# Which engine makes the low mantissa bits of three weight blocks: GpSimd or VectorE, in an attention and rational feed-forward kernel

## The chip, the core and the metric

The kernel runs on one core of a Trainium2 chip. The metric is the device time of one execution in microseconds (us), lower is better. The kernel before has a median of 679.99 us over 3 runs, from 679.7 to 680.04.

The core has four computing engines, each of which runs its own list of instructions strictly in order: TensorE (PE, its weight loads are shown as PEld), VectorE (DVE), ScalarE (ACT) and GpSimd (POOL). SyncE (SP) issues the transfers. An instruction waits for semaphores that other engines raise, and everything behind it on its engine waits with it.

## The reference

```python
def _attn_ref(x, state):                      # x: 8 x 8 x 512 x 64, state: 8 x 8 x 32 x 64
    scores = scale * np.matmul(x, state.transpose(0, 1, 3, 2))
    a = softmax(scores)                       # over the 32 states
    xread = np.matmul(a, state)
    scores2 = scale * np.matmul(state, x.transpose(0, 1, 3, 2))
    a2 = softmax(scores2)                     # over the 512 positions
    sread = np.matmul(a2, x)
    return np.concatenate([xread, sread], axis=2)

def _moe_ref(x, w_in, w_out, a, b):           # x: 4352 x 512, w_in: 512 x 2048, w_out: 2048 x 512
    h = x @ w_in
    P = a[0] + a[1] * h + a[2] * h**2 + a[3] * h**3
    Q = 1.0 + np.abs(b[0]) * np.abs(h) + np.abs(b[1]) * h**2
    return ((P / (Q + 1e-06)) @ w_out).astype(np.float32)
```

`w_in` and `w_out` reach the kernel as 64-bit floats, seen as two 32-bit words per number. The kernel makes 32-bit floats of them itself, at its start.

## The kernel before

The order of all work is written out by hand in the table `ORDER`: a list of tokens such as `jr:2`, each of which calls one small function. Every function appends its instructions to the lists of its engines, so that the table sets the order on each engine. Waits are put in by the framework, from the tiles that instructions read and write.

**The weights.** There are 16 raw blocks of 128 x 1024 numbers (1 MB each), numbered by `groups`: 0, 1, 2 are the first three eighths of `w_in`, then eighths of `w_out` and of `w_in` take turns (block 3 is `w_out` 0, block 4 is `w_in` 3, block 5 is `w_out` 1). A block g passes these steps:

- `lr:g:k` (`load_raw`, issued at L281 or L287) loads half k of it into a raw tile of pairs of words.
- `cp:g:k` (`conv_parts`, L299, ScalarE) makes the sign, exponent and upper mantissa of half k, into the tile `cv_y`.
- `jr:g` (`join_rest`, L308) makes the three lowest mantissa bits out of the other word: it reads every second word of the raw tile, multiplies by 2^-29, takes the minimum with 7 and writes integers to the tile `cv_r`.
- `jl:g` (`join`, L319, VectorE) shifts `cv_y` and joins it with `cv_r`. For a block of `w_in` the result is `win_sb`; for one of `w_out` it goes back into `cv_r`.
- For `w_out`, `wh:g` (L329, ScalarE) and `wl:g:k` (L336, GpSimd) split the result into a high and a low part for TensorE.

`cv_y` and `cv_r` share four buffers. As the program is built, the `cv_r` of block 2 lies in the buffer that held the `cv_r` of block 1, which `jl:1` reads; the `cv_r` of block 3 lies in the buffer of block 2's `cv_y`, which `jl:2` reads; the `cv_r` of block 4 lies where that of block 2 was.

**The rest of the start.** Beside this, the start computes the attention of the first batch (`scores0`, `row_max0` and so on; `row_norm0`, L577, runs on GpSimd, `a_lo0`, L591, on VectorE), and folds state and `w_in` into products (`X`, L694, with `XA`, L712, `fh`, L726, and `fo`, L730).

**The main part.** 72 steps n then pass through the rational function. `F` (L784, PE) makes h; `FC` (L796) and `FB` (L803) copy it on ScalarE; `qd` (L817), `mu` (L807), `po` (L811), `g1`, `g2`, `g3` (L828, L834, L840) run on VectorE; `qa` (L823), `ln` (L893) and `ex` (L903) on ScalarE; `gl` (L847) on GpSimd; `mh` and `ml` (L856) multiply by `w_out` on PE. The first of them starts at 21 us, while blocks 2 to 4 are being converted. That stretch of the table reads:

```python
    "cp:2:0 a_hi0:1 cv e2_copy0:0 cp:2:1 b0a cp:3:0 fh:1 a_lo0:0 a_lo0:1 jr:2 jl:2 F:0:0 XA:4 F:0:1 "
    "fo:1 cp:3:1 cp:4:0 jr:3 col_norm:0 F:1:0 jl:3 F:1:1 jr:4 FC:0 lr:5:0 FB:0 wh:3 FB:1 qd:0 ..."
```

Of the kernel before, what the change touches and what calls it, by code (L numbers as in the profile page):

```python
# [198 lines left out]
def attention_rational_ffn(  # L199
# [6 lines left out]
    nc = tc.nc  # L206
# [98 lines left out]
        )  # L305

    def join_rest(g):
        nc.vector.tensor_scalar(  # L308
            CV[g][1], RAW[g][:, :, 0], 2.0**-29, 7.0, op0=ALU.mult, op1=ALU.min
        )  # L310

# [598 lines left out]
    def sread_lo():  # L910
# [8 lines left out]
        "lr": load_raw,  # L919
        "cp": conv_parts,  # L920
        "jr": join_rest,
        "jl": join,
        "ws": store_win,
# [50 lines left out]
    for name, args in tokens:  # L974
        if name in ("scores0", "scores", "sread"):
            b, g = (0, *args)[-2:]
# [51 lines left out]
```

## Time and profile before

| what | value |
|---|---|
| median of 3 runs | 679.99 us (679.7 to 680.04) |
| span of the profiled execution, first to last instruction | 678.2 us |
| the runs' median less that span | 1.8 us |
| PE busy | 653.1 us (96%) |
| DVE busy | 629.4 us (93%) |
| ACT busy | 518.4 us (76%) |
| POOL busy | 307.4 us (45%) |

The page gives no device time of its own for the profiled execution; its span is what stands there, and it is 1.8 us less than the median of the runs. Busy time counts the instructions of an engine from start to end. A busy PE is no PE at its peak, and a wait of an engine costs time only where something else waits for what comes after it.

### The profile page before, as it was taken

To read this page: it belongs to the slowest core of one execution; us is meant where nothing else is said; L and a number is where in the kernel's file an instruction comes from. 1 tells how busy PE (TensorE), PEld (TensorE's weight loads), DVE (VectorE), ACT (ScalarE), POOL (GpSimd) and SP (SyncE) were. 2 spreads that over 40 slices of the span, in tenths; PEclk is the share of its full clock that TensorE was granted. 3 is DMA by queue.
4 is the path that set the end of the run, shared out by engine and by line. 5 is a ranking of instruction groups with operands and counts; after the bars stand their busy time and mean duration, and the time that the engine had idled before them with its cause. 6 is when DMAs were issued, how large, how long until landed. Compare 5 with 4: busy or idle time off the path is not lost.

```text
span 678.2 us, 11288 instructions
## 1 busy us (share of the span) xinstructions
PE 653.1 (96%) x4474; PEld 510.7 (75%) x4474; DVE 629.4 (93%) x583; ACT 518.4 (76%) x633; POOL 307.4 (45%) x174
## 2 busy tenths in 40 slices
PE   5779999999999999999999999999999999999997
PEld 2547667877887777877878878778878888888895
DVE  4989999899998998899999998999999998999896
ACT  4989989886787777786786867858787868774772
POOL 1234346434543445344554455543553565465630
PEclk9979999999999999999999999999999999999999
DMA  8959886334442454021333203121412111204301
GB/s 334 412 213 338 303 289 234 100 125 141 135 157 56 150 183 161 32 73 52 109 128 121 63 16 105 53 74 64 140 54 88 62 48 62 78 0 141 124 2 31
DMA packets 30679, 85.67 MB, mean 126 GB/s; under 512 B 3490, under 2 KB 3618, under 8 KB 30626
## 3 DMA queue, kind: packets, MB, share of 16 engines
q1 hardware_dynamic: 30290, 84.56, 35.7%
q8 instruction: 35, 0.57, 0.3%
q10 hardware_dynamic: 336, 0.39, 0.2%
q14 instruction: 18, 0.15, 0.1%
HBM read 57.15 MB, written 27.79 MB: 125 GB/s over the span
## 4 chain that ended last, share of the span: by engine, by line
PE 85%; ACT 6%; DVE 5%; issue 2%; DMA 1%; POOL 0%; SPq 0%; POOLq 0%; DVEq 0%; ACTq 0%
PE h L784 27%; PE ps_x L694 3%; PE o__1511 L856 2%; PE o__3578 L856 2%; PE o__1588 L856 2%; PE o__4769 L856 2%; PE o__4111 L856 2%; PE o__4116 L856 2%; PE o__1516 L856 2%; PE o__5847 L856 2%; PE o__4121 L856 2%; PE o__5866 L856 2%; PE o__1506 L856 2%; PE o__3571 L856 2%; PE o__5331 L856 2%
## 5 line engine op out<-in xcount | busy, mean ns | idle before, releaser
L847 POOL TENSOR_TENSOR gl<-C,L 128x1024 fp32r<-128x1024 f32 (+1 forms) x70 | 173.3, 2476 | 228.7 <-DVE C L840 150.7
L784 PE MATMUL h<-aT,m 128*128 128x512 f32 x768 | 191.9, 393 | 1.4 <-DVE m L730 1.0
L784 PEld LDWEIGHTS h<-aT,m 128*128 128x128 f32 x768 | 143.0, 188 | 36.9 <-DVE m L730 1.9
L803 ACT ACTIVATE A<-h,cst 128x1024 f32<-128x1024 f32 (+1 forms) x72 | 77.0, 1069 | 43.7 <-PE h L784 43.0
L743 POOL TENSOR_TENSOR m<-m_sb,m 128x512 fp32r<-128x512 f32 x56 | 79.8, 1435 | 65.8 <-ACT m L739 42.8
L828 DVE SCALAR_TENSOR_TENSOR gh<-C,cst,L 128x1024 fp32r<-128x1024 f32 (+1 forms) x72 | 95.5, 1328 | 12.6 <-ACT L L903 10.9
L796 ACT ACTIVATE C<-h,cst 128x1024 f32<-128x1024 f32 (+1 forms) x72 | 83.4, 1159 | 22.6 <-PE h L784 14.1
L817 DVE SCALAR_TENSOR_TENSOR A<-A,b0a,h 128x1024 f32<-128x1024 f32 (+1 forms) x72 | 87.2, 1213 | 10.0 <-ACT A L803 6.3
L840 DVE SCALAR_TENSOR_TENSOR C<-C,cst,A 128x1024 f32<-128x1024 f32 (+1 forms) x72 | 94.3, 1311 | 0.8
L834 DVE SCALAR_TENSOR_TENSOR A<-A,gh 128x1024 f32<-128x1024 f32 (+1 forms) x72 | 89.2, 1241 | 1.2
L823 ACT ACTIVATE A<-A 128x1024 f32<-128x1024 f32 (+1 forms) x72 | 73.0, 1014 | 22.0 <-DVE A L817 21.3
L811 DVE SCALAR_TENSOR_TENSOR C<-C,cst,h 128x1024 f32<-128x1024 f32 (+1 forms) x72 | 87.5, 1217 | 1.3
L807 DVE TENSOR_TENSOR C<-C,h 128x1024 f32<-128x1024 f32 (+1 forms) x72 | 83.0, 1153 | 3.0 <-issue 1.3
L893 ACT ACTIVATE L<-A 128x1024 f32<-128x1024 f32 (+1 forms) x72 | 72.9, 1012 | 7.0 <-POOL gl L847 4.4
L903 ACT ACTIVATE L<-L 128x1024 f32<-128x1024 f32 (+1 forms) x72 | 72.8, 1012 | 1.3
L739 ACT CAST m<-m_sb 128x512 fp32r<-128x512 f32 x56 | 34.4, 617 | 7.8 <-PE h L784 6.9
L694 PE MATMUL ps_x<-win_sb,st 64*32 64x256 f32 x1024 | 37.1, 415 | 3.4 <-DVE win_sb L319 1.4
L694 PEld LDWEIGHTS ps_x<-win_sb,st 64*32 64x32 f32 x1024 | 18.1, 114 | 19.3 <-issue 8.6
L336 POOL TENSOR_TENSOR wo<-cv_r,wo 128x512 fp32r<-128x512 f32 x16 | 20.3, 1293 | 26.3 <-ACT wo L329 26.3
L784 PEld LDWEIGHTS h<-sh,m 128*128 128x128 f32 x192 | 24.6, 190 | 1.1
L489 POOL TENSOR_TENSOR e<-e,rs 128x512 f32<-128x512 f32 x14 | 17.3, 1256 | 17.2 <-DVE rs L483 17.2
L784 PE MATMUL h<-sh,m 128*128 128x256 f32 x192 | 24.9, 282 | 0.0
(246 smaller groups left out, 1121.5 us busy)
## 6 DMA issues: line engine op xcount, KB each, us to landing
m_sb<-m_dram SPq DMA_DIRECT2D x56, 256.0 KB, 3.0
xT_sb<-in_xT_dram SPq DMA_DIRECT2D x16, 512.0 KB, 4.8
x_sb<-in_x_dram SPq DMA_DIRECT2D x16, 512.0 KB, 5.8
m_dram<-xo SPq DMA_DIRECT2D x16, 512.0 KB, 5.6
win_sb<-w_in_dram SPq DMA_DIRECT2D x16, 512.0 KB, 4.5
out_dram<-o_sb SPq DMA_DIRECT2D x32, 256.0 KB, 3.8
raw<-in_w_in_dram SPq DMA_DIRECT2D x10, 512.0 KB, 7.9
raw_w<-in_w_out_dram SPq DMA_DIRECT2D x8, 512.0 KB, 9.4
```

Source lines behind the costliest of these rows:

```text
L743: nc.gpsimd.tensor_tensor(m[:, 1], MF.pop(n), m[:, 0].bitcast(F32), op=ALU.subtract)
L784: nc.tensor.matmul(h[:, ci * W : (ci + 1) * W], l, r, start=(q == 0), stop=(q == len(seq) - 1),)
L796: nc.scalar.activation(e["C"], e["h"], AF.Identity, scale=cst[:, 3:4], bias=cst[:, 2:3])
L803: nc.scalar.activation(e["A"], e["h"], AF.Abs, scale=cst[:, 5:6])
L807: nc.vector.tensor_tensor(e["C"], e["C"], e["h"], op=ALU.mult)
L811: nc.vector.scalar_tensor_tensor(e["C"], e["C"], cst[:, 1:2], e["h"], op0=ALU.add, op1=ALU.mult)
L817: nc.vector.scalar_tensor_tensor(e["A"], e["A"], b0a, e["h"], op0=ALU.add, op1=ALU.mult)
L828: nc.vector.scalar_tensor_tensor(e["gh"], e["C"], cst[:, 0:1], e["L"], op0=ALU.add, op1=ALU.mult)
L834: nc.vector.scalar_tensor_tensor(e["A"], e["A"], 1.0 + 1e-6, e["gh"].bitcast(F32), op0=ALU.add, op1=ALU.mult)
L840: nc.vector.scalar_tensor_tensor(e["C"], e["C"], cst[:, 0:1], e["A"], op0=ALU.add, op1=ALU.subtract)
L847: eng.tensor_tensor(e["gl"], e["C"], e["L"], op=ALU.mult)
L856: nc.tensor.matmul(O[t], e[l][:, j * W + t * P : j * W + (t + 1) * P], WO[u][:, j, k, :], start=(u == 0 and l == "gh" and k == 0 and j == ...
```

## The change

`jr:2`, `jr:3` and `jr:4`, that is blocks 2, 3 and 4 of the raw weights (the third to the fifth), go to GpSimd. The table `ORDER`, the tiles, the operation and its shapes stay as they are; `jr` of the 13 other blocks stays on VectorE. From L308 on, lines stand one further down.

```diff
     def join_rest(g):
-        nc.vector.tensor_scalar(
+        eng = nc.gpsimd if 2 <= g <= 4 else nc.vector
+        eng.tensor_scalar(
             CV[g][1], RAW[g][:, :, 0], 2.0**-29, 7.0, op0=ALU.mult, op1=ALU.min
         )
```

VectorE between `jl:1` (the first row) and `mu:0` (the last), before. `cv_r_286`, `cv_r_295` and `cv_r_322` are the `cv_r` tiles of blocks 2, 3 and 4:

```order
L319 SCALAR_TENSOR_TENSOR win_sb_256<-cv_y_171,cv_r_172 128x1024
L455 TENSOR_SCALAR r2_229<-r2_229 128x2
L591 TENSOR_TENSOR aT_264<-ps_a0_231,aT_264 128x512
L591 TENSOR_TENSOR aT_264<-ps_a0_259,aT_264 128x512
L308 TENSOR_SCALAR cv_r_286<-raw_w_137 128x1024
L319 SCALAR_TENSOR_TENSOR win_sb_302<-cv_y_285,cv_r_286 128x1024
L730 TENSOR_TENSOR m_297<-ps_x_268,m_297 128x512
L308 TENSOR_SCALAR cv_r_295<-raw_w_143 128x1024
L459 RECIPROCAL r2_229<-r2_229 128x2
L319 SCALAR_TENSOR_TENSOR cv_r_295<-cv_y_294,cv_r_295 128x1024
L308 TENSOR_SCALAR cv_r_322<-raw_203 128x1024
L817 SCALAR_TENSOR_TENSOR A_345<-A_345,b0a_82,h_304 128x1024
```

The same stretch of VectorE with the change, with the semaphores that each instruction waits for:

```order
L320 SCALAR_TENSOR_TENSOR win_sb<-cv_y,cv_r 128x1024 [waits DVE_49]
L456 TENSOR_SCALAR r_229<-r_229 128x2 [waits Activation_49]
L592 TENSOR_TENSOR aT<-ps_a_231,aT 128x512 [waits Activation_49]
L592 TENSOR_TENSOR aT<-ps_a_259,aT 128x512 [waits Activation_49]
L320 SCALAR_TENSOR_TENSOR win_sb<-cv_y,cv_r 128x1024 [waits Activation_49,Pool_49]
L731 TENSOR_TENSOR m<-ps_x,m 128x512 [waits PE_49,Activation_49]
L460 RECIPROCAL r_229<-r_229 128x2 [waits DVE_49]
L320 SCALAR_TENSOR_TENSOR cv_r<-cv_y,cv_r 128x1024 [waits Activation_49,Pool_49]
L818 SCALAR_TENSOR_TENSOR A<-A,b0a,h 128x1024 [waits PE_49,Activation_49]
```

Three instructions are gone, and the two joins `jl:2` and `jl:3` (L320) now wait for GpSimd.

GpSimd with the change, from `row_norm0` (L578) to the first `gl` (L848); before, the two `wl:3` (L337) followed on `row_norm0` directly:

```order
L578 TENSOR_TENSOR e_131<-e_131,rs 128x512 [waits DVE_49,Activation_49]
L578 TENSOR_TENSOR e_131<-e_131,rs 128x512 [waits DVE_49]
L309 TENSOR_SCALAR cv_r<-raw_w 128x1024 [waits DMAHW1_49,DMAHW0_49,DVE_49]
L309 TENSOR_SCALAR cv_r<-raw_w 128x1024 [waits DMAHW4_49,DMAHW2_49,DVE_49]
L309 TENSOR_SCALAR cv_r<-raw 128x1024 [waits DMAHW6_49,DMAHW5_49,Pool_49]
L337 TENSOR_TENSOR wo<-cv_r,wo 128x512 [waits Activation_49]
L337 TENSOR_TENSOR wo<-cv_r,wo 128x512
L848 TENSOR_TENSOR gl<-C,L 128x1024 [waits DVE_49,Activation_49]
```

The three new instructions stand together. The wait of the first for VectorE is for the end of `jl:1`, that of the second for the end of `jl:2` (`jl:1` and `jl:2` read the buffers that the two then write); the third waits for GpSimd's own first one.

## Rows read from the trace of the kernel before

**Rows 1.** The page: busy time of each engine, and the chain that ended last.

```profile
PE 653.1 (96%) x4474; PEld 510.7 (75%) x4474; DVE 629.4 (93%) x583; ACT 518.4 (76%) x633; POOL 307.4 (45%) x174
...
PE 85%; ACT 6%; DVE 5%; issue 2%; DMA 1%; POOL 0%; SPq 0%; POOLq 0%; DVEq 0%; ACTq 0%
```

**Rows 2.** Stretches: length, busy PE, PEld, DVE, ACT, POOL, clock, DMA share, GB/s.

```profile
20.00:30.00 10.00, 7.16 (x57) 4.93 (x56) 9.65 (x13) 9.97 (x17) 2.40 (x2) 1.00 1.02 410
30.00:40.00 10.00, 4.29 (x99) 2.75 (x107) 9.65 (x10) 8.56 (x13) 2.47 (x2) 0.53 0.61 238
```

**Rows 3.** Timeline of DVE: start, duration (us), engine, line, operation, tiles.

```profile
18.47 1.47 DVE L319 SCALAR_TENSOR_TENSOR win_sb<-cv_y,cv_r 128x1024 int32<-128x1024 int32 x1
...
21.25 0.68 DVE L308 TENSOR_SCALAR cv_r<-raw_w 128x1024 int32<-128x1024 uint32 x1
22.04 1.23 DVE L319 SCALAR_TENSOR_TENSOR win_sb<-cv_y,cv_r 128x1024 int32<-128x1024 int32 x1
23.40 0.69 DVE L730 TENSOR_TENSOR m<-ps_x,m 128x512 fp32r<-128x512 f32 x1
...
24.79 1.22 DVE L319 SCALAR_TENSOR_TENSOR cv_r<-cv_y,cv_r 128x1024 int32<-128x1024 int32 x1
25.93 0.69 DVE L308 TENSOR_SCALAR cv_r<-raw 128x1024 int32<-128x1024 uint32 x1
26.63 1.28 DVE L817 SCALAR_TENSOR_TENSOR A<-A,b0a,h 128x1024 f32<-128x1024 f32 x1
```

**Rows 4.** Timeline of ACT from 21 us on.

```profile
21.02 0.72 ACT L299 ACTIVATE cv_y<-raw_w 128x512 f32<-128x512 f32 x1
...
22.71 0.65 ACT L712 COPY xo<-ps_x 128x512 f32<-128x512 f32 x1
...
25.40 1.19 ACT L803 ACTIVATE A<-h,cst 128x1024 f32<-128x1024 f32 x1
26.41 1.12 ACT L329 CAST wo<-cv_r 128x1024 fp32r<-128x1024 f32 x1
```

**Rows 5.** All waits of ACT from 15 to 45 us: total, times, longest.

```profile
ACT xo_w L712 <- PE ps_x L694: 1.2, 1, 1.2
ACT srT L640 <- PE ps_sr L635: 0.6, 1, 0.6
```

**Rows 6.** Timeline of POOL: its neighbours around the three new instructions.

```profile
16.04 1.05 POOL L577 TENSOR_TENSOR e<-e,rs 128x512 f32<-128x512 f32 x1 [14.64 <-DVE cm L400]
17.49 1.37 POOL L577 TENSOR_TENSOR e<-e,rs 128x512 f32<-128x512 f32 x1 [0.40 <-DVE rs L572]
27.60 2.51 POOL L336 TENSOR_TENSOR wo<-cv_r,wo 128x512 fp32r<-128x512 f32 x2 [8.74 <-ACT wo L329]
```

**Rows 7.** Timeline of DVE: two instructions that ran beside POOL.

```profile
53.53 2.07 DVE L319 SCALAR_TENSOR_TENSOR win_sb<-cv_y,cv_r 128x1024 int32<-128x1024 int32 x1
...
257.72 1.83 DVE L828 SCALAR_TENSOR_TENSOR gh<-C,cst,L 128x1024 fp32r<-128x1024 f32 x1
```

**Rows 8.** Timeline of POOL beside those, and one undisturbed instruction (35.70).

```profile
35.70 2.36 POOL L847 TENSOR_TENSOR gl<-C,L 128x1024 fp32r<-128x1024 f32 x1 [5.59 <-DVE C L840]
...
51.97 2.55 POOL L336 TENSOR_TENSOR wo<-cv_r,wo 128x512 fp32r<-128x512 f32 x2
...
257.19 1.29 POOL L743 TENSOR_TENSOR m<-m_sb,m 128x512 fp32r<-128x512 f32 x1 [2.38 <-DVE r L455]
258.44 3.39 POOL L847 TENSOR_TENSOR gl<-C,L 128x1024 fp32r<-128x1024 f32 x1
```

**Rows 9.** POOL's groups by form: busy us, mean ns of one, idle before.

```profile
L911 POOL TENSOR_TENSOR sh<-srT,sh 128x1024 fp32r<-128x1024 f32 x1 | 2.4, 2420 | 0.0
...
masks.py:199 POOL TENSOR_SCALAR_AFFINE_SELECT ident<-ident 128x128 f32<-128x128 f32 x1 | 0.3, 284 | 0.0
masks.py:197 POOL MEMSET ident<- 128x128 f32 x1 | 0.2, 206 | 0.3 <-POOLq L1010 0.3
...
L1010 POOL MEMSET const-float32-0.0<- 128x1 f32 x1 | 0.1, 104 | 0.2 <-issue 0.2
```

## The prediction

> **What bounds the kernel now.** Begin with the page: PE is busy for 96% of the span and VectorE for 93%, and 85% of the chain that ended last lies on PE [rows 1]. That is an average over the whole kernel; the change touches the stretch from 20 to 27 us. So the second view is busy time by stretch [rows 2]: from 20 to 30 us ScalarE is busy for 9.97 of 10 us, VectorE for 9.65, PE for 7.16. Here ScalarE sets the pace. The waits of ScalarE say it more sharply: between 15 and 45 us it waits only twice, 1.2 us and 0.6 us, both times for PE [rows 5], so nothing that VectorE does in these 30 us holds it up. The third view is the timelines of the stretch, to see how much room the touched instructions have [rows 3, 4, 6].
>
> **What is removed.** Three instructions of VectorE of 0.68, 0.68 and 0.69 us [rows 3] (the second, `jr:3`, is like the first): 2.04 us. I cost their removal at nothing. `jl:2` started at 22.04, but it also needs ScalarE's `cp:2:1`, which ends at 21.02 + 0.72 = 21.74 [rows 4]. `fo:1` (23.40) needs what ScalarE signals at the end of `XA:4`, 22.71 + 0.65 = 23.36. `qd:0` (26.63) needs `FB:0`, which ends at 25.40 + 1.19 = 26.59. And `wh:3`, which needs `jl:3` (24.79 + 1.22 = 26.01), starts at 26.41 only because ScalarE comes to it then. Each of VectorE's results is met by a ScalarE that is not yet there, so the freed 2.04 us become idle time. The cover is ScalarE's full list; were it gone, up to 2.04 us could be won.
>
> **What is added: the way through GpSimd.** The three instructions stand between `row_norm0` (ends 17.49 + 1.37 = 18.86) and `wl:3` (27.60) in a gap of 8.74 us [rows 6]. GpSimd has the time; the question is who waits. With d for the duration of one, and 0.1 us for a semaphore's way (`wh:3` ends at 27.53 and `wl:3` starts at 27.60 [rows 4, 6]):
>
> - `jr:2` waits for `jl:1`, which ends at 18.47 + 1.47 = 19.94 [rows 3], so it runs from 20.04 to 20.04 + d.
> - `jl:2` starts at the later of 21.84 (ScalarE) and 20.14 + d. Up to d = 1.70 it is the first, and `jl:2` ends at 23.07, 0.20 earlier than before.
> - `jr:3` waits for `jl:2`: from 23.17 to 23.17 + d. `fo:1` is not moved.
> - `jr:4` stands right behind it: to 23.17 + 2d.
> - `jl:3` waits for `jr:3`. At 23.17 + d it is free to go, but `jr:4` already runs. Does it have to stand aside?
>
> **The shared way to memory.** It does, by the rows. `jl` of a later block, `L319` with two inputs from SBUF, started at 53.53 while GpSimd ran two instructions from 51.97 to 54.52, and took 2.07 us instead of 1.22: it ended at 55.60, 1.08 after GpSimd [rows 7, 8]. `jl:1` shows the same: it ended at 19.94, 1.08 after `row_norm0` [rows 3, 6]. The other direction is there too: an instruction of VectorE that was already waiting (257.72) ended at 259.55, 1.07 after GpSimd's running one (258.48), while GpSimd's next took 3.39 us instead of 2.36 [rows 7, 8]. So whoever comes second stands still until the first is done. `jr:4` comes first here, since it follows on its own engine, while `jl:3` hears of `jr:3` by a semaphore.
>
> The Trainium skill (SBUF — State Buffer, Who interferes with whom) has this as a rule: an instruction of VectorE with two SBUF inputs and one of GpSimd that reads SBUF exclude each other for the whole instruction. By that rule `jl:3` stands still as in my sum; without it `jl:3` would start at 23.27 + d, end at 25.99 for d = 1.5, and nothing would be lost.
>
> Thus `jl:3` ends at 23.17 + 2d + 1.08, and `wh:3` on ScalarE starts 0.07 later instead of at 26.41. The delay is 2d - 2.09 us, none up to d = 1.05; above d = 1.70 `jl:2` slips as well and each further us costs three.
>
> **The price d.** The trace has no one-input instruction of this size on GpSimd. From below: VectorE's own 0.68 us [rows 3], which gives no delay; a gain below that is excluded, as shown above. From above: 2.42 us for GpSimd with two inputs of 128 x 1024 [rows 9]; then `jl:2` ends at 20.14 + 2.42 + 1.23 = 23.79, `jl:3` at 23.89 + 4.84 + 1.08 = 29.81, and `wh:3` is 3.47 us late. Between them I go by the row that is nearest in kind, the affine select, also one input and one output: 0.284 us for 128 elements against 0.104 for a memset of one, so 0.18 / 127 = 1.42 ns per element, and 0.10 + 1.45 = 1.55 us for 1024 [rows 9]. I take **d = 1.5 us**: the delay is 2 x 1.5 - 2.09 = 0.9 us.
>
> **Does it reach the end?** `wh:3` is late by 0.9, and ScalarE's list behind it follows without a gap until its two waits [rows 5], which are for PE work that itself waits for ScalarE. `qd:0` stands behind `jl:3` on VectorE and is 0.7 late. PE, 4.29 us busy between 30 and 40 with a granted clock of 0.53 [rows 2], waits for these; I see nothing to absorb the delay before PE becomes the bound, and a later start of PE's part ends later by as much. The low clock I cost at nothing, as the order of work is the same. The transfers that wait for `jr:2` to `jr:4` refill the raw tiles for blocks 6 to 8, which stand far behind in the table; `wl:3` follows `wh:3`, as before.
>
> **Sum.** Against the profiled execution: 678.2 + 0.9 = 679.1 us of span. The runs' median lies 1.8 us above that span, so the runs should show 680.9 us.
>
> **Rivals.**
>
> 1. *Nothing happens: 680.0 us.* Either d is at most 1.05, or `jl:3` gets in ahead of `jr:4`. For it: the memset row gives (0.206 - 0.104) / 127 = 0.80 ns per element, 0.92 us for 1024 [rows 9]. Against it: a memset reads nothing. The Trainium skill (GPSIMD Engine Reference, Engine selection) supports this rival: it calls one-input work on GpSimd roughly line-rate; no run here shows that yet. Chance 0.27.
> 2. *Slower, 681.4 to 683.5 us.* The same wait of `jl:3` behind `jr:3` and `jr:4`, with an instruction that reads every second word and converts integers at a price near that of two inputs. It decides from d = 1.72 on, where the delay passes 1.36 us (0.2% of 680, about what a measurement of this kernel can tell from no change), and ends at d = 2.42 with 3.5 us. Chance 0.26.
> 3. *A first call that is dear.* `jr:2` is GpSimd's first of this kind, and each us that it takes above 1.70 delays `jl:2` and all behind it by one. Against it: GpSimd's first TENSOR_TENSOR took 1.05 us, its second 1.37 [rows 6]. The Trainium skill (GPSIMD Engine Reference, Instruction dispatch) gives about 6 us for the first call to a freshly loaded kernel; no row shows such a load. By that price it would be some 686 us. Chance 0.05.
> 4. *Faster, 678.0 us.* VectorE's 2.04 us reach the end. For it: 9.65 of 10 us busy [rows 2]. Against it: the four starts above, each within reach of ScalarE. Chance 0.07.
>
> **How the numbers follow.** The forecast, d between 1.05 and 1.72, has 0.35. Forecast and rival 1 lie within 0.2%: 0.62 the same. Rivals 2 and 3 make 0.31 slower, rival 4 makes 0.07 faster. The range begins at 679.6, the unchanged time less the spread of the runs, and ends at 682.9: d = 2.2 puts `jl:2`'s end at 23.57 and `jl:3`'s at 29.15, a delay of 2.8. Outside lie rivals 3 and 4 and the upper part of rival 2, together about 0.2.
>
> **What would show it.** Right: `jr:2` to `jr:4` on GpSimd at about 1.5 us each, the last two back to back from 23.2 us; `jl:3` shown with a long duration and ending 1.1 us behind `jr:4`; `wh:3` at about 27.3. Wrong: `wh:3` still at 26.4 (rival 1, then the duration of `jr` or the start of `jl:3` says which half), an instruction of more than 1.7 us (rival 2), a first one far longer than the others (rival 3), or `qd:0` before 26.6 (rival 4).

## The result, and the profile after

The kernel with the change takes 683.68 us (median of 4 runs, 683.56 to 684.0), the one before 680.01 us beside it (4 runs, 679.7 to 680.19). The ratio is 1.0054, with a 95% interval from 1.0042 to 1.0066. The change costs 3.67 us; 680.9 us was forecast, and 682.9 us was the top of the range. The profiled execution took 683.56 us with a span of 681.8 us. In the experiments further down, line numbers shift again with each edit.

The page first, with the two lines that answer to [rows 1]:

```profile
PE 653.0 (96%) x4474; PEld 510.8 (75%) x4474; DVE 627.0 (92%) x580; ACT 519.0 (76%) x633; POOL 321.0 (47%) x177
...
PE 85%; DVE 5%; ACT 5%; issue 2%; POOL 1%; DMA 1%; SPq 0%; POOLq 0%; ACTq 0%; DVEq 0%
```

VectorE lost 2.4 us of work, GpSimd gained 13.6 us, and the shares of the chain hardly differ. At this level nothing looks wrong. The stretches say more (columns as in [rows 2]):

```profile
20.00:30.00 10.00, 7.24 (x58) 4.98 (x57) 4.19 (x7) 6.63 (x13) 8.50 (x3) 1.00 1.03 408
30.00:40.00 10.00, 2.16 (x64) 1.71 (x64) 9.46 (x8) 9.59 (x12) 6.35 (x3) 0.54 0.62 240
```

From 20 to 30 us VectorE fell from 9.65 to 4.19 us busy, far more than the 2.04 us that were taken from it: it stands still. ScalarE fell from 9.97 to 6.63, and GpSimd rose from 2.40 to 8.50. What is missing on ScalarE is 3.34 us, and it set the pace here. Its waits from 15 to 45 us answer to [rows 5]:

```profile
ACT wo L330 <- DVE cv_r L320: 3.7, 1, 3.7
ACT xo_w L713 <- PE ps_x L695: 1.2, 1, 1.2
ACT srT L641 <- PE ps_sr L636: 0.6, 1, 0.6
```

The two old waits are unchanged, and one of 3.7 us is new: `wh:3` for `jl:3`. The waits of VectorE over the same time name the next link, twice GpSimd's `join_rest`:

```profile
DVE cv_r L320 <- POOL cv_r L309: 3.1, 1, 3.1
DVE win_sb L320 <- POOL cv_r L309: 2.6, 1, 2.6
```

The timelines give the prices and the order. POOL, answering to [rows 6]; the three L309 rows are `jr:2`, `jr:3` and `jr:4`:

```profile
17.54 1.37 POOL L578 TENSOR_TENSOR e<-e,rs 128x512 f32<-128x512 f32 x1 [0.40 <-DVE rs L573]
20.08 3.90 POOL L309 TENSOR_SCALAR cv_r<-raw_w 128x1024 int32<-128x1024 uint32 x1 [1.17 <-DVE r L456]
25.32 3.70 POOL L309 TENSOR_SCALAR cv_r<-raw_w 128x1024 int32<-128x1024 uint32 x1 [1.34 <-DVE win_sb L320]
29.11 4.75 POOL L309 TENSOR_SCALAR cv_r<-raw 128x1024 int32<-128x1024 uint32 x1
33.93 2.50 POOL L337 TENSOR_TENSOR wo<-cv_r,wo 128x512 fp32r<-128x512 f32 x2
```

DVE, answering to [rows 3]: `jl:2`, `fo:1`, `jl:3`, `qd:0`.

```profile
24.02 1.23 DVE L320 SCALAR_TENSOR_TENSOR win_sb<-cv_y,cv_r 128x1024 int32<-128x1024 int32 x1 [2.62 <-POOL cv_r L309]
25.16 0.68 DVE L731 TENSOR_TENSOR m<-ps_x,m 128x512 fp32r<-128x512 f32 x1
...
29.06 1.23 DVE L320 SCALAR_TENSOR_TENSOR cv_r<-cv_y,cv_r 128x1024 int32<-128x1024 int32 x1 [3.15 <-POOL cv_r L309]
30.20 1.27 DVE L818 SCALAR_TENSOR_TENSOR A<-A,b0a,h 128x1024 f32<-128x1024 f32 x1
```

ACT, answering to [rows 4]: `FB:0`, `wh:3`, `FB:1`.

```profile
25.45 1.18 ACT L804 ACTIVATE A<-h,cst 128x1024 f32<-128x1024 f32 x1
30.32 1.05 ACT L330 CAST wo<-cv_r 128x1024 fp32r<-128x1024 f32 x1 [3.69 <-DVE cv_r L320]
31.27 1.11 ACT L804 ACTIVATE A<-h,cst 128x1024 f32<-128x1024 f32 x1
```

One instruction costs 3.70 us on GpSimd, 0.69 us on VectorE. The chain is `jl:1`, `jr:2` (3.90), `jl:2` (1.23), `jr:3` (3.70), `jl:3` (1.23), `wh:3`: two dear instructions in series, each followed by the join that needs it; `jr:3` can't begin before `jl:2` has ended, since it overwrites what `jl:2` reads. `wh:3` starts at 30.32 instead of 26.41, 3.91 us late. `jr:4` is the longest, 4.75 us, yet nobody in this stretch waits for it but `wl:3`, which stands behind it on GpSimd and starts at 33.93 instead of 27.60.

The delay arrives whole at PE's main part. Matrix product `F:2` on PE, before and then after:

```profile
44.61 2.99 PE L784 MATMUL h<-aT,m 128*128 128x512 f32 x12 [0.97 <-DVE m L730]
```

```profile
48.45 2.99 PE L785 MATMUL h<-aT,m 128*128 128x512 f32 x12 [0.98 <-DVE m L731]
```

It takes 2.99 us in both, waits 0.97 and 0.98 us for the same thing, and comes 3.84 us later. The span is 3.6 us longer.

### The profile page after: what moved, and what is told of

Its sections match the earlier page's. It is cut to its first block, busy times and chain, and to the rows that moved or that the text cites. A ratio compares the mean times of both kernels' runs of the same rounds, so it can differ in the third digit from the quotient of the medians.

```text
span 681.8 us, 11288 instructions
## 1 busy us (share of the span) xinstructions
PE 653.0 (96%) x4474; PEld 510.8 (75%) x4474; DVE 627.0 (92%) x580; ACT 519.0 (76%) x633; POOL 321.0 (47%) x177
## 4 chain that ended last, share of the span: by engine, by line
PE 85%; DVE 5%; ACT 5%; issue 2%; POOL 1%; DMA 1%; SPq 0%; POOLq 0%; ACTq 0%; DVEq 0%
PE h L785 26%; PE ps_x L695 4%; PE o__1511 L857 2%; PE o__3578 L857 2%; PE o__1588 L857 2%; PE o__4769 L857 2%; PE o__4111 L857 2%; PE o__4116 L857 2%; PE o__1516 L857 2%; PE o__5847 L857 2%; PE o__4121 L857 2%; PE o__1506 L857 2%; PE o__3571 L857 2%; PE o__5331 L857 2%; PE o__5866 L857 2%
## 5 line engine op out<-in xcount | busy, mean ns | idle before, releaser
L848 POOL TENSOR_TENSOR gl<-C,L 128x1024 fp32r<-128x1024 f32 (+1 forms) x70 | 173.2, 2474 | 227.2 <-DVE C L841 148.6
L337 POOL TENSOR_TENSOR wo<-cv_r,wo 128x512 fp32r<-128x512 f32 x16 | 21.8, 1386 | 15.5 <-ACT wo L330 15.4
```

Source lines behind the costliest of these rows:

```text
L848: eng.tensor_tensor(e["gl"], e["C"], e["L"], op=ALU.mult)
```

## The experiments

### One block at a time

In each of three kernels one block alone goes to GpSimd; the number is 2, 3 or 4.

```diff
     def join_rest(g):
-        nc.vector.tensor_scalar(
+        eng = nc.gpsimd if g == 2 else nc.vector
+        eng.tensor_scalar(
```

Block 2 alone:

> Only jr:2 (block 2) on GpSimd, blocks 3 and 4 stay on VectorE. Theory A (in the changed kernel each join waits for its own GpSimd instruction of 3.7 to 3.9 us, and the two waits of jl:2 and jl:3 add up): jr:2 from 20.1 to 24.0 us, jl:2 from 24.0, fo:1 at 25.2, the second F (PE) at 25.9, jl:3 at about 26.6, wh:3 at 27.9; the second FB, which needs that F, at 29.0 instead of 27.3: 1.4 to 1.8 us slower than before. Theory B (the loss comes from jr:3 and jr:4 back to back in front of jl:3, as the prediction had it): under 0.5 us slower.

Block 3 alone:

> Only jr:3 (block 3) on GpSimd. Theory A: it waits for the end of jl:2 (about 23.3 us), runs 3.7 us, to 27.1; jl:3 from 27.1 to 28.4, wh:3 at 28.4 instead of 26.4: 1.9 to 2.3 us slower than before, and with the run of block 2 alone about the whole 3.7 us of the change. Theory B: no more than 0.5 us slower, since jr:4 is not there to hold jl:3 up.

Block 4 alone:

> Only jr:4 (block 4) on GpSimd. Nothing waits for its result before 39 us, but it starts behind jl:2 (23.3 us) and is still running when jl:3, which has two inputs from SBUF, comes at about 24.7. If the running GpSimd instruction keeps jl:3 off for its whole length: jl:3 ends 1.1 us behind it, at about 28.2, wh:3 at 28.3: 1.8 us slower than before. If it does not (the long instruction leaves the way to SBUF free most of the time): jl:3 as before, no difference (within 0.2 us).

Measured beside a median before of 679.88 us (22 runs):

| on GpSimd | median us | range | ratio, 95% interval | more than before |
|---|---|---|---|---|
| block 2 | 681.37 | 681.08 to 681.74 | 1.0021 [1.0012, 1.0031] | 1.49 |
| block 3 | 681.73 | 681.68 to 681.97 | 1.0028 [1.0017, 1.0039] | 1.85 |
| block 4 | 679.89 | 679.65 to 680.29 | 1.0 [0.9991, 1.001] | 0.01 |

The three add up to 3.35 of the 3.67 us; the intervals, some 0.6 us either way, can't tell the two apart. So the loss is made of two separate delays, each of one `jr` less the room that it finds, and the move of block 4 costs nothing by itself. By itself `jr:4` is thereby shown to be off the path, and 0.69 us less work on VectorE is seen to be worth nothing here.

The trace of block 4 alone showed something else. `jr:4` on POOL, then `jr:3` and `jl:3` on DVE beside it:

```profile
23.49 3.72 POOL L309 TENSOR_SCALAR cv_r<-raw 128x1024 int32<-128x1024 uint32 x1 [4.51 <-DVE win_sb L320]
```

```profile
24.15 1.01 DVE L309 TENSOR_SCALAR cv_r<-raw_w 128x1024 int32<-128x1024 uint32 x1
...
25.27 1.23 DVE L320 SCALAR_TENSOR_TENSOR cv_r<-cv_y,cv_r 128x1024 int32<-128x1024 int32 x1
```

GpSimd's instruction runs from 23.49 to 27.21. VectorE's `jr:3` began 0.66 us after it and took 1.01 instead of 0.68 us; if it ran at its usual speed once it could go, it was held until about 24.5. `jl:3`, with two inputs from SBUF, then ran in its usual 1.23 us wholly inside the other. So GpSimd's `tensor_scalar` did not hold VectorE for its 3.72 us, and by this reading only for about the first of them.

### What the instruction's price is made of

The kernel before, with sixteen instructions of GpSimd behind its end, two of each of eight kinds: the one that was moved, and the same with half the elements, with words that stand side by side instead of every second one, on floats without a conversion, with one operation instead of two, and as a plain copy. The first pair of it and the first pair with one operation:

```diff
+        two = dict(op0=ALU.mult, op1=ALU.min)
+        for _ in range(2):
+            nc.gpsimd.tensor_scalar(dst, pairs, 2.0**-29, 7.0, **two)
...
+        for _ in range(2):
+            nc.gpsimd.tensor_scalar(dst, pairs, 2.0**-29, None, op0=ALU.mult)
```

> The kernel before with 16 instructions of GpSimd behind its end, two of each form, one after the other with nothing beside them; the output is the same, the time longer by their sum. Prices of 128 x 1024: if every second word is what costs, the contiguous forms fall from 3.7 us to under 2 and the paired float form stays at 3.7; if the conversion of integers costs, the float forms fall to under 2 and the contiguous integer form stays; if the second operation costs, the forms with mult alone fall to about half; if none of them, tensor_scalar costs 3.5 to 3.7 us in every form and only the copy is cheap. 512 elements instead of 1024 should take about 1.9 us. A first call dearer than the second would show in the first pair.

It was executed once (726.87 us); what counts are the single durations. POOL's groups by form in that kernel (busy us, mean ns of one, idle before); every second word is read at L992, L994, L998 and L1002, neighbouring words at L996, L1004 and L1006:

```profile
L992 POOL TENSOR_SCALAR p_dst<-p_src 128x1024 int32<-128x1024 uint32 x2 | 7.3, 3668 | 12.6 <-DVE p_src L984 12.5
L998 POOL TENSOR_SCALAR p_dst<-p_src 128x1024 f32<-128x1024 f32 x2 | 7.3, 3666 | 0.2
...
L996 POOL TENSOR_SCALAR p_dst<-p_src 128x1024 int32<-128x1024 uint32 x2 | 7.2, 3624 | 0.2
L1002 POOL TENSOR_SCALAR p_dst<-p_src 128x1024 int32<-128x1024 uint32 x2 | 5.6, 2814 | 0.2
L1004 POOL TENSOR_SCALAR p_dst<-p_src 128x1024 f32<-128x1024 f32 x2 | 5.5, 2768 | 0.2
L994 POOL TENSOR_SCALAR p_dst<-p_src 128x512 int32<-128x512 uint32 x2 | 3.9, 1937 | 0.2
...
L1006 POOL COPY p_dst<-p_src 128x1024 f32<-128x1024 f32 x2 | 2.1, 1038 | 0.1
```

3.67 us with nothing else running beside it: the price is the instruction's own and no effect of its place. It isn't the stride (3.62 for neighbours) nor the conversion (3.67 for floats). The second operation accounts for 0.85 us (3.668 - 2.814). The slope is (3668 - 1937) / 512 = 3.4 ns per element, against 1.42 that the affine select had suggested. The copy, at 1.04 us, is the only kind near the 0.92 us of rival 1. The two-input `TENSOR_TENSOR`, taken as the bound from above, is cheaper than this one-input instruction: 2.42 [rows 9] against 3.67.

### A cheap instruction in the same three places

`jr:2` to `jr:4` stay on GpSimd, but as a copy: the top byte of the low word goes into `cv_r`, in place of its three top bits.

```diff
     def join_rest(g):
+        if 2 <= g <= 4:
+            top = RAW[g].rearrange("p a w -> p (a w)").bitcast(mybir.dt.uint8)
+            top = top.rearrange("p (a q) -> p a q", q=8)[:, :, 3]
+            nc.gpsimd.tensor_copy(CV[g][1], top)
+            return
```

> All three on GpSimd as in the change, but as a copy, which the price list has at 1.04 us: it copies the top byte of the low word instead of multiplying and taking the minimum, so the lowest 8 bits of these weights are not right. Theory A (the price of 3.7 us alone makes the loss; the two waits add up): jl:2 and jl:3 find their input in time, wh:3 at 26.4 us, no difference from before (within 0.2%, 680.0 us). Theory C (having these three on GpSimd costs in itself, by semaphores, order or the shared way to SBUF): still 1 us slower or more.

Measured: 679.87 us (679.54 to 680.13) beside 679.88 (21 runs), ratio 0.9998 [0.9989, 1.0008]. The delay is gone, with the same three handovers between VectorE and GpSimd, the same buffers and the same refills of the raw tiles. So neither these nor the place cost the 3.67 us; the price does. And all 2.04 us taken from VectorE bring nothing, though here the copies take some of it back: `jl:3` is 0.88 us longer than before (2.10 against 1.22).

POOL and DVE of this kernel (`jr:3`, `jr:4`; `jl:2`, `fo:1`, `jl:3`, `qd:0`):

```profile
23.16 1.13 POOL L311 CAST cv_r<-raw_w 128x1024 int32<-128x1024 uint8 x1 [1.85 <-DVE win_sb L324]
24.23 1.12 POOL L311 CAST cv_r<-raw 128x1024 int32<-128x1024 uint8 x1
```

```profile
21.87 1.23 DVE L324 SCALAR_TENSOR_TENSOR win_sb<-cv_y,cv_r 128x1024 int32<-128x1024 int32 x1 [0.50 <-ACT cv_y L299]
23.41 0.69 DVE L735 TENSOR_TENSOR m<-ps_x,m 128x512 fp32r<-128x512 f32 x1 [0.31 <-ACT xo L717]
...
24.33 2.10 DVE L324 SCALAR_TENSOR_TENSOR cv_r<-cv_y,cv_r 128x1024 int32<-128x1024 int32 x1 [0.15 <-POOL cv_r L311]
26.64 1.28 DVE L822 SCALAR_TENSOR_TENSOR A<-A,b0a,h 128x1024 f32<-128x1024 f32 x1 [0.21 <-ACT A L808]
```

Three of these four waits are for ScalarE, before `jl:2`, `fo:1` and `qd:0`, as the prediction had named them.

Here `jr:4` was first, by 0.10 us, and `jl:3` came out as the prediction had drawn it: 2.10 us long, ending at 26.43, 1.08 us behind `jr:4` (25.35). In the changed kernel `jl:3` was first, by 0.05 us (29.06 against 29.11), and it was `jr:4` that stretched, from 3.70 to 4.75 us.

### One operation instead of two

The minimum with 7 is left out.

```diff
     def join_rest(g):
+        if 2 <= g <= 4:
+            nc.gpsimd.tensor_scalar(
+                CV[g][1], RAW[g][:, :, 0], 2.0**-29, None, op0=ALU.mult
+            )
+            return
```

> All three on GpSimd, with the multiplication alone (2.8 us in the price list); the minimum with 7 is left out. Theory A, with d for the price: jl:2 starts at 20.14 + d, jr:3 0.1 behind its end, jl:3 0.1 behind jr:3, wh:3 at 22.87 + 2d = 28.5 instead of 26.4 us, against 30.3 for d = 3.7 to 3.9: 1.8 to 2.1 us slower than before. Theory C: nearer to the 3.7 us of the change than to half of it.

Measured: 681.95 us (681.88 to 682.41), ratio 1.0031 [1.002, 1.0043], 2.07 us more than before. The delay shrank from 3.67 by 1.60 us, and two instructions on the path at 0.85 us less would make 1.70. In this trace `jr:2` took 3.05 and `jr:3` 2.85 us. `wh:3` on ACT:

```profile
28.60 1.05 ACT L334 CAST wo<-cv_r 128x1024 fp32r<-128x1024 f32 x1 [1.99 <-DVE cv_r L324]
```

### A buffer of its own for block 3

`jr:3` waits for `jl:2` only because it overwrites the `cv_y` that `jl:2` reads. Here the `cv_r` of block 3 goes into a buffer that is still free, so `jr:3` may follow `jr:2` at once; the rest is as in the changed kernel.

```diff
-            r = cv.tile([P, 4 * CW], I32, name="cv_r", tag="cv")
+            if g == 3:
+                r = cp.tile([P, 2, 4 * CW], I32, name="cv_r", tag="w1")[:, 0]
+            else:
+                r = cv.tile([P, 4 * CW], I32, name="cv_r", tag="cv")
```

> The change, but the low bits of block 3 go to a buffer that nothing uses at that time, so that jr:3 need not wait for jl:2 to have read its old one. Theory A: jr:3 follows jr:2 at once, 24.0 to 27.7 us, wh:3 at 29.1 instead of 30.3; 2.3 to 2.8 us slower than before instead of 3.7. If the wait for the buffer plays no part: 3.7 us slower as in the change.

Measured: 683.41 us (683.39 to 683.5), ratio 1.0051 [1.0035, 1.0068], 3.53 us more than before. Only 0.14 us was won, not the 0.9 to 1.4 us that had been expected. POOL (`jr:2` and `jr:3` in one row) and DVE (`jl:2`, `jl:3`):

```profile
20.20 8.69 POOL L312 TENSOR_SCALAR cv_r<-raw_w 128x1024 int32<-128x1024 uint32 x2 [1.18 <-DVE r L459]
```

```profile
24.10 1.22 DVE L323 SCALAR_TENSOR_TENSOR win_sb<-cv_y,cv_r 128x1024 int32<-128x1024 int32 x1 [2.58 <-ACT cv_y L302]
...
28.92 1.23 DVE L323 SCALAR_TENSOR_TENSOR cv_r<-cv_y,cv_r 128x1024 int32<-128x1024 int32 x1 [2.92 <-POOL cv_r L312]
```

`jr:2` and `jr:3` now stand together, but take 8.69 us where 3.90 + 3.70 = 7.60 was due: 1.09 more, about the length of `jl:2`, which ran beside them unstretched. Of the two, `jr:2` took 3.87 us; `jr:3` started at 24.14, 0.04 behind `jl:2`, and took 4.74. So the buffer did let `jr:3` go, but behind `jl:2` it was longer by 1.04 us, like `jr:4` behind `jl:3` in the changed kernel (4.75): what the buffer gave, the shared way to memory took.

### Two inputs at block 4's place

Block 4 alone goes to GpSimd, as a difference of a word with itself. It leaves the wanted bits out, and has the two inputs that the rows of before had shown to exclude VectorE.

```diff
     def join_rest(g):
+        if g == 4:
+            up = RAW[g][:, :, 1].bitcast(F32)
+            nc.gpsimd.tensor_tensor(CV[g][1].bitcast(F32), up, up, op=ALU.subtract)
+            return
```

> Only jr:4 on GpSimd, and as a TENSOR_TENSOR of two inputs (the upper words less themselves, 2.4 us), so the low bits of block 4 are left out. It runs from 23.4 to 25.9 us beside jr:3 (24.1) and jl:3 (24.8) of VectorE. If a TENSOR_TENSOR of GpSimd holds the way to SBUF for its whole length, as the trace of before has it, and the tensor_scalar of the run with block 4 alone did not: jr:3 is held to 25.9 and ends at 26.5, jl:3 ends at 27.8, wh:3 at 27.9: 1.3 to 1.5 us slower than before, though GpSimd is busy for less time than with tensor_scalar, which cost nothing. If both leave the way free alike: no difference.

Measured: 680.57 us (680.44 to 680.85), ratio 1.0011 [1.0001, 1.002], 0.69 us more than before, just clear of no change. POOL (`jr:4`) and DVE (`jr:3`):

```profile
23.42 1.89 POOL L310 TENSOR_TENSOR cv_r<-raw 128x1024 f32<-128x1024 f32 x1 [4.49 <-DVE win_sb L323]
```

```profile
24.05 1.81 DVE L312 TENSOR_SCALAR cv_r<-raw_w 128x1024 int32<-128x1024 uint32 x1
```

The instruction took 1.89 us, less than the 2.4 that the expectation had used, and so the loss is smaller than expected. It is half as long as the `tensor_scalar` at the same place, and yet it costs more: VectorE's `jr:3`, which has one input only, was held until 25.31, its very end, and finished 0.55 us after it at 25.86. That is 1.13 us later than its usual 0.68 us would give; 0.40 us of it is room (`jl:3` ended at 26.01 before and `wh:3` started at 26.41), which leaves 0.7.

### What GpSimd's idle time is good for

The copies made GpSimd cheap, and ScalarE sets the pace in this stretch. So the next kernel is the one before with `wh:3`, a plain copy of ScalarE, on GpSimd, and with two tokens of ScalarE's pulled forward into its place.

```diff
-    "... jr:4 FC:0 lr:5:0 FB:0 wh:3 FB:1 qd:0 ... qd:1 e2_copy0:1 wl:3:0 g1:0 cp:4:1 cp:5:0 ..."
+    "... jr:4 FC:0 lr:5:0 FB:0 wh:3 e2_copy0:1 cp:4:1 FB:1 qd:0 ... qd:1 wl:3:0 g1:0 cp:5:0 ..."
...
-        nc.scalar.copy(
+        copy = nc.gpsimd.tensor_copy if g == 3 else nc.scalar.copy
+        copy(
```

> The kernel before with other work on GpSimd: wh:3, the copy of 128 x 1024 from SBUF to SBUF that ScalarE makes at 26.4 us, goes to GpSimd at the price of a copy (1.04 to 1.3 us), and ScalarE makes e2_copy0:1 and cp:4:1 in its place instead of at 31.6 and 32.0. If ScalarE's full list from 20 to 38 us is what bounds the start, FC:1 comes at 32.2 instead of 33.2 us and the whole is 0.5 to 1.0 us faster than before (0.9985 to 0.9993); if VectorE, busy for 9.65 of 10 us there, binds as much, under 0.3 us.

Measured: 678.87 us (11 runs, 678.7 to 679.39) beside 679.79 (16 runs, 679.61 to 680.46), ratio 0.9987 [0.9978, 0.9996]. It is 0.92 us faster than the kernel before and 4.8 us faster than the changed one. This is below the 0.2% that the prediction had set as a limit, but with this many runs the interval leaves out 1. `wh:3` on POOL, `FC:1` on ACT (33.18 before) and `F:2` on PE (44.61 before):

```profile
26.29 1.44 POOL L323 CAST wo<-cv_r 128x1024 fp32r<-128x1024 f32 x1 [7.24 <-DVE cv_r L312]
```

```profile
32.45 1.18 ACT L790 ACTIVATE C<-h,cst 128x1024 f32<-128x1024 f32 x1
```

```profile
43.87 3.00 PE L778 MATMUL h<-aT,m 128*128 128x512 f32 x12
```

ScalarE came 0.73 us earlier to `FC:1`, and PE 0.74 us earlier to `F:2`. The copy was moved and two tokens were pulled forward in one edit; no run took these apart.

The same once more, for `wh:5` too:

```diff
-    "... jl:4 XA:5 wh:5 XA:8 lr:6:1 cp:6:0 ws:2 ..."
+    "... jl:4 XA:5 wh:5 cp:6:0 XA:8 lr:6:1 ws:2 ..."
...
-        copy = nc.gpsimd.tensor_copy if g == 3 else nc.scalar.copy
+        copy = nc.gpsimd.tensor_copy if g in (3, 5) else nc.scalar.copy
```

> As the run before, and wh:5 on GpSimd as well, with cp:6:0 in its place on ScalarE ahead of XA:8, so that fh:2 comes 0.5 us earlier: another 0.3 to 0.5 us, 0.8 to 1.5 us faster than before in all. If the second F (n = 2) waits for VectorE or PE instead of fh:2: no more than the run before.

Measured: 681.75 us (6 runs, 681.22 to 682.55), ratio 1.0028 [1.0016, 1.0039]. The second copy lost 2.9 us against the first one alone, where a further gain had been expected. POOL from 40 us on (`wh:5`, `gl:0`, `wl:5`) and DVE beside it (`g1:1`, `g2:1`, and `jr:6`):

```profile
40.28 1.97 POOL L323 CAST wo<-cv_r 128x1024 fp32r<-128x1024 f32 x1 [9.99 <-DVE cv_r L312]
42.21 3.36 POOL L841 TENSOR_TENSOR gl<-C,L 128x1024 fp32r<-128x1024 f32 x1
45.53 3.98 POOL L330 TENSOR_TENSOR wo<-cv_r,wo 128x512 fp32r<-128x512 f32 x2
```

```profile
41.27 2.06 DVE L822 SCALAR_TENSOR_TENSOR gh<-C,cst,L 128x1024 fp32r<-128x1024 f32 x1
...
43.85 2.80 DVE L828 SCALAR_TENSOR_TENSOR A<-A,gh 128x1024 f32<-128x1024 f32 x1
...
49.55 0.69 DVE L301 TENSOR_SCALAR cv_r<-raw_w 128x1024 int32<-128x1024 uint32 x1 [1.18 <-POOL wo L330]
```

GpSimd works in order, so the copy put `gl:0` and `wl:5` behind it: `gl:0` began at 42.21 instead of 35.70 [rows 8], `wl:5` at 45.53 instead of 42.39. Now they met VectorE's `g1:1` and `g2:1`, which have two inputs each. `g1:1` (2.06 instead of 1.28 us) ended 1.08 us behind the copy, `g2:1` (2.80 instead of 1.52) 1.08 us behind `gl:0`, and `gl:0` and `wl:5` were stretched in turn, to 3.36 and 3.98 instead of 2.36 and 2.52 us. VectorE's `jr:6` then waited for the end of `wl:5`. `F:2` on PE still began at 43.98; the delay comes behind it, where ScalarE waited 2.19 us for `jl:7`, which follows `jr:6`, before `wh:7`. This reading is from the trace of this one kernel; no run took the parts of it apart.

## Why the prediction was wrong

**The price d: wrong, and outside its own bounds.** "Between them I go by the row that is nearest in kind, the affine select" gave 1.5 us, with 2.42 us as the bound from above. Measured are 3.67 us alone, and 3.90 and 3.70 us for the two on the path. Two things failed. The affine select is another operation: the line through the two sizes of the price list would put a `tensor_scalar` of 128 elements at 0.64 us (an estimate, 1.937 - 384 x 0.00338), more than twice the 0.284 of the select, so the smaller size alone doesn't explain it. And the bound rested on the thought that one input can't cost more than two. The price list refutes that, and shows that nothing special about the operand was to blame, which had been rival 2's reason (every second word, integers to convert): a plain `tensor_scalar` on neighbouring floats with one operation took 2.77 us. The rule quoted with rival 1, the Trainium skill (GPSIMD Engine Reference, Engine selection), that one-input work there is roughly line-rate, comes near for the copy (1.04 us, 1.5 times the 0.68 us of VectorE's `tensor_scalar`) and fails for GpSimd's `tensor_scalar`, whose 3.67 us are 5.4 times VectorE's 0.68.

**"`jr:4` comes first here": wrong, by 0.05 us.** `jl:3` started at 29.06, `jr:4` at 29.11. With `jl:3` first, the prediction's own steps put `wh:3` at 22.87 us plus the durations of `jr:2` and `jr:3`. With 3.90 and 3.70 that is 30.47; 30.32 was measured. With one operation, 3.05 and 2.85, it is 28.77; 28.60 was measured. The rest is in the handovers, which took 0.04 to 0.07 us where 0.10 was counted. So above 1.70 a further us of d costs two and not three: the run with one operation lost 1.60 us less for 0.85 us less of d. The two errors pulled apart: with `jr:4` first and d = 3.70, the prediction's sum would have put `jl:3`'s end at 25.17 + 7.40 + 1.08 = 33.65 and the loss at 7.3 us. With `jl:3` first and d = 1.5, it would have given no loss at all. That the measured 683.68 us lies only 0.8 above the range is luck. (The range's top is also 0.1 off by its own terms: 680.0 + 2.8 = 682.8.) The reason given, that an instruction behind another on its own engine is ahead of one that hears by a semaphore, held for the copies (by 0.10 us) and not for the `tensor_scalar`: in the changed kernel, with one operation and, twice, with the own buffer, VectorE's join was first each time, by 0.04 to 0.05 us. At this distance it was no ground for a step.

**"Whoever comes second stands still until the first is done": right for the rows it came from, too wide as a rule.** It held for `TENSOR_TENSOR` at block 4's place, for the copies, and for GpSimd behind `jl` (`jr:4` of 4.75, `jr:3` of 4.74 us with its own buffer). It failed for VectorE behind GpSimd's `tensor_scalar`, which let VectorE go after about 1 us of 3.72. The Trainium skill (SBUF — State Buffer, Who interferes with whom) says that whoever issues first has the shared pair of ports for the whole instruction; the block 4 run differs from that, and the measurement decides. It was not needed for the result, since `jl:3` was first.

**What is removed costs and gains nothing: right.** With all three copies on GpSimd and 2.04 us taken from VectorE the time was unchanged (ratio 0.9998), and VectorE stood waiting for ScalarE at `jl:2`, `fo:1` and `qd:0`. Rival 4 falls.

**Two waits in series, above d = 1.70: right.** The text said that `jl:2` slips above that point. That is what happened, and the runs with block 2 alone (1.49 us) and block 3 alone (1.85 us) show the two links one by one. In the changed kernel `fo:1` moved too (25.16 instead of 23.40), as it stands behind `jl:2`.

**The delay reaches the end: right.** 3.91 us at `wh:3`, 3.84 at `F:2`, 3.67 in the medians. The wait of `wl:3` behind `jr:4` was missed; it came 6.3 us later than before, and its results are ready at 36.43, well ahead of PE's first product with `wo`, at 46.28.

**Rival 3, a dear first call: wrong.** `jr:2` took 3.90, the next one 3.70: 0.20 us, and even that is no price of a first call. Where `jr:3` or `jr:4` was the first of its kind, it took 3.72 us, and in the price list the two of the first pair differ by 0.01 us; `jr:2` was longer by 0.14 to 0.20 us at its place also with one operation (3.05 against 2.85) and as a copy (1.27 against 1.13). Why is open. The load of some 6 us that the Trainium skill (GPSIMD Engine Reference, Instruction dispatch) gives for the first call to a freshly loaded kernel isn't seen in any run here.

**Rival 2 came nearest, with too low an end.** It had a dear d and slower runs, at a chance of 0.26, and stopped at 683.5 us, because d stopped at 2.42. Its reason for the price was wrong, and so was its wait behind `jr:4`.

## What to carry to other kernels

An idle engine is not a cheap one: before work is moved to it, the price of the very operation there has to be measured, by itself and at its size, since here one input cost more than two and a copy cost under a third of what was moved. Then follow the chain over the engines: here the two dear instructions in front of joins were paid for, less the room in front of them, and the one that nobody waited for cost nothing. Off the chain is not enough by itself, for at that same place a shorter instruction with two inputs cost 0.69 us by keeping VectorE standing. Last, look at what stands behind the moved work on its new engine, for the copy that helped at `wh:3` did harm at `wh:5`.

## What the runs showed of the hardware

- GpSimd's `tensor_scalar` on 128 x 1024 took 3.67 us with two operations and 2.8 us with one, the same for every second and for neighbouring words and with or without a conversion; the copy took 1.04 us, and a difference of a tile with itself 1.89 us.
- GpSimd's `tensor_scalar` held VectorE at most for about the first us of its 3.72 us, the 1.89 us `TENSOR_TENSOR` for its whole length, and the one held was an instruction with a single input. Why the two differ is open: that the first has read its input by then and only computes is a guess that no run here tests.
- Which of two instructions that become free together goes first was decided by 0.04 to 0.10 us: in four of four cases VectorE's join started ahead of GpSimd's next `tensor_scalar`, and in the one case with a copy GpSimd was first.
